# Loads of u issued by GpSimd instead of SyncE, and new costs in the planner of a fused attention and MoE kernel

## The chip, the cores and the metric

The kernel runs on one core of one Trainium2 chip. The metric is the device time of one execution in microseconds (us): the median of three runs. One further execution was taken with the hardware profiler; all rows of "the profile" and "the trace" are of that execution.

## The reference, cut to what matters

```python
# u, v: (8, 3008, 256); z: (8, 3008, 64); w_in: (256, 2048); w_out: (2048, 256)
scores = (z @ z.T) / S                     # per batch, S = 3008: a symmetric matrix
attn   = np.maximum(scores, 0.0) ** 2
x      = u * (attn @ v)                    # (8, 3008, 256)
x      = x.reshape(8 * 3008, 256)          # 24064 tokens
h      = x @ w_in
out    = (h * sigmoid(1.702 * h)) @ w_out  # (24064, 256), float32
```

## The kernel before, in words

**Units and tiles.** The attention half is cut into 48 units: 8 batches of 6 blocks of 512 rows (the last block of a batch has 448). The MoE half is cut into 47 tiles m of 512 tokens. In TensorE's order, tile m follows the attention work of unit m + 3.

**Work of a unit n.** `scores` makes 128 x 512 blocks of z z^T, two at a time (one pair, in PSUM, L340). Each pair is passed through relu (ScalarE L373 or VectorE L375) and squared in place (ScalarE L357 or VectorE L359) into a tile `ap_`. `values` multiplies V with the squares into four PSUM banks O (L553); h = 0 and h = 1 are the two halves of the 256 columns. Since the scores are symmetric, a square made for one unit serves a later unit transposed: SyncE issues a DMA transpose, `T<-ap_` (L295). From the second batch on, a part of a unit's own diagonal block is also made by such a transpose, the "mirror" (`ap_<-ap_`, L310).

**Draining.** `both_sums` copies two banks to one of five `sums` buffers (ScalarE L531, VectorE L533) and GpSimd adds the two halves (L526). A `sums` buffer of O is free again when the gate has read it; one of the MoE output, when its store to DRAM has landed. Each unit takes two buffers for O and each tile m two for the output, in a strict rotation of five.

**The steps of u.** For each unit u is loaded as float32 into `RU` (L96, issued by SyncE in `load_u`), split by GpSimd into its 16-bit halves (`UH<-RU`, L138), transposed by two DMA transposes that SyncE issues (`UHT<-UH`, L142) and merged by GpSimd (`UT<-UHT`, L146). There is one buffer of each, so the load of the next unit waits for the split of this one. The gate on GpSimd (`XT<-sums,UT`, L564, one for each h) multiplies the added sums with UT and gives the input of the MoE half. SyncE then swaps its partition halves (`XS<-XT`, L440); `hidden` (L596) needs both. `outs` (L639) makes the output.

**MoE elementwise work.** ScalarE makes the sigmoid `tsg<-hg` (L603), VectorE the product `GT<-hg,tsg` (L607).

**What sets the order.** Every engine carries out its own list of instructions in order; semaphores join the lists. The order in the lists is written by a planner inside the kernel: it walks through TensorE's work and keeps a clock for each engine (`now`), a table of costs (`cost`) and due times. `push` offers an operation for one or several engines: the one that would finish it first takes it, the earliest start goes first, and of equal starts the kinds in FIRST ("part", "gate", "add", "merge") go first. `send` offers a transfer to SyncE's list, which takes those that are ready by the number of the unit they are due for. `ready` times after a DMA are the issue's end plus `T_DMA`. `at(n, j, ...)` in the main part fixes the place of loads of weights, z and V on GpSimd by a position in unit n; before each a small copy, `hold`, makes GpSimd wait for the newest square. The planner knows nothing of the rotation of the `sums` buffers.

The first batch starts without any squares to reuse, loads all weights, and makes z and V of the second batch ready; from the second batch on all batches look alike.

Of the kernel before, what the change touches and what calls it, by code (L numbers as in the profile page):

```python
# [15 lines left out]
def kernel(  # L16
# [97 lines left out]

    def load_u(n):
        b, isup = divmod(n, NIS)
        rows(b, u, isup, 1, RU, sp, False)

    def load_z(b):
        for k in range(NIS):  # L120
# [33 lines left out]
    def turn_z(b, q):  # L154

        c = slice(q * ZN, (q + 1) * ZN)
        pool.tensor_copy(z16[:, c, 1, :], z16[:, c, 0, :])  # L157

        def turn(at):
            sp.dma_start_transpose(ZT[b % 2][:, c, :], z16[:, c, :, :].rearrange("p n a d -> p (n a d)"))  # L160
            if q == ZQ - 1:
                z_at[b] = at + T_DMA

        send(now["pe"] + 1.0, "turn_z", b * NIS - 3, turn)

# [5 lines left out]
    NU = B * NIS  # L171
    v_at = [7.2, 9.5, 10.0, 13.0, 13.5, 15.5]
    T_SC, T_SW, T_MM, T_HG = 0.215, 0.1, 0.107, 0.215
    T_LAT, T_SEM, T_DMA = 0.25, 0.1, 3.5
    now = {"pe": 6.0, "act": 6.0, "dve": 7.0, "pool": 6.0, "sp": 6.0}
    cost = {
        ("act", "relu"): 1.03, ("dve", "relu"): 1.23, ("act", "sq"): 1.03, ("dve", "sq"): 0.95,
        ("act", "keep"): 0.6, ("dve", "keep"): 0.45, ("act", "keep2"): 1.03, ("dve", "keep2"): 0.75,
        ("act", "relu_half"): 0.6, ("dve", "relu_half"): 0.7, ("act", "sq_half"): 0.6, ("dve", "sq_half"): 0.42,
        ("act", "part"): 0.6, ("dve", "part"): 0.7, ("pool", "add"): 1.1, ("act", "sig"): 1.03, ("dve", "gt"): 1.23, ("pool", "gate"): 1.2,  # L180
        ("sp", "turn"): 1.45, ("sp", "mirror"): 1.3, ("pool", "split"): 2.2, ("pool", "merge"): 2.2, ("sp", "turn_u"): 2.9, ("sp", "turn_z"): 2.2, ("sp", "store"): 0.6, ("sp", "swap"): 1.2,
    }
    BOTH = ("act", "dve")
    FIRST = ("part", "gate", "add", "merge")
    ops = []
    pushed = 0
# [4 lines left out]
    def push(ready, kind, engines, fn):  # L191
        nonlocal pushed
        pushed += 1
        ops.append((ready, pushed, kind, engines, fn))
# [4 lines left out]
    def advance(t):  # L199

        while ops:
            best = None
            for o in ops:
                e = min(o[3], key=lambda x: max(now[x], o[0]) + cost[(x, o[2])])
                key = (max(now[e], o[0]), o[2] not in FIRST, o[2][:2] == "sq", o[1])
                if best is None or key < best[0]:
                    best = key, o, e
            (start, *_), o, e = best
            if start > t:
                break  # L210
            ops.remove(o)
            now[e] = start + cost[(e, o[2])]
            o[4](e, now[e] + T_SEM)
        while now["sp"] <= t:
            can = [o for o in sends if o[0] <= t and (o[4] is None or o[4]())]
            if not can:
                break
            o = min(can, key=lambda o: (o[2], o[0]))
            sends.remove(o)
            now["sp"] = max(now["sp"], o[0]) + cost[("sp", o[1])]  # L220
            o[3](now["sp"])

    def pe_at(rows_, dur):
# [7 lines left out]
    NDIR = 3  # L231
# [52 lines left out]
    def turn(n, t, at):  # L284

        b, isup = divmod(n, NIS)
        key = (b * NIS + t // 2, isup)
        if key not in T:
            c = colors.pop(0)
            T_col[key] = c  # L290
            T[key] = ptp.tile([P, NIB, NIB, P], F16, name=f"T{c}", tag=f"T{c}")
            T_left[key] = [2, NIB]
        a = A[(n, t)]
        g0 = (t % 2) * 2
        sp.dma_start_transpose(  # L295
            T[key][:, g0:g0 + 2, :, :].rearrange("p g i r -> p (g i) r"), a.rearrange("p g c -> p (g c)"),
        )
        T_left[key][0] -= 1
        if T_left[key][0] == 0:
            T_at[key] = at + T_DMA  # L300
        a_left[(n, t)] -= 1

    def by_halves(a):
# [3 lines left out]
    def mirror(n, at):  # L307

        t = n % NIS * 2
        sp.dma_start_transpose(  # L310
            A[(n, t + 1)].rearrange("p g (i r) -> p (g i) r", i=NIB)[:, :NIB, :],
            A[(n, t)].rearrange("p g c -> p (g c)")[:, ISUP:],
        )
        a_left[(n, t)] -= 1
        half_at(n, at + T_DMA)

    halves_at = {}

# [6 lines left out]
    def scores(k):  # L325

        nonlocal nxt
        for i in range(k):
            n, t = pairs[nxt]
            nxt += 1  # L330
            b, isup = divmod(n, NIS)
            Z = ZT[b % 2]
            assert b in z_at
            p_ = take_ps()
            sc = psA.tile([P, 2, ISUP], F32, name="sc", tag="A")
            low = NIB // 2 if mirrored(n, t) else 0
            cols = slice(low * P, ISUP)
            for g in range(2):
                h0 = g * DQK
                pe.matmul(  # L340
                    sc[:, g, cols], Z[h0:h0 + DQK, 2 * t + g, :],
                    Z[h0:h0 + DQK, isup * NIB + low:(isup + 1) * NIB, :],
                    start=True, stop=True,
                )
            part = "_half" if low else ""
            if (n, t) in home:
                a = home[(n, t)]
            else:
                a = pap.tile([P, 2, ISUP], F16, name="ap_", tag="ap_")
                ring.append((n, t))  # L350
            A[(n, t)] = a
            a_left[(n, t)] = 2 + (turns(n, t) or mirrored(n, t + 1))

            def squared(e, at, n=n, t=t, a=a, isup=isup, cols=cols):
                x = by_halves(a)[:, :, 1, :] if mirrored(n, t) else a
                if e == "act":
                    act.activation(x, x, AF.Square, scale=1.0)  # L357
                else:
                    dve.tensor_tensor(x, x, x, ALU.mult)  # L359
                if mirrored(n, t):  # L360
                    half_at(n, at)
                else:
                    A_at[(n, t)] = at
                    if mirrored(n, t + 1):
                        send(at, "mirror", n - 1, lambda at: mirror(n, at), lambda: (n, t + 1) in A)
                latest[0] = a
                if turns(n, t):
                    key = (n - isup + t // 2, isup)
                    send(at, "turn", NDIR if n == 1 and (n, t) in home else key[0], lambda at: turn(n, t, at), lambda: key in T or len(colors) > 0)

            def relu(e, at, p_=p_, x=sc, y=a, part=part, squared=squared):
                if e == "act":
                    act.activation(y, x, AF.Relu, scale=CSC)  # L373
                else:
                    dve.tensor_scalar(y, x, 0.0, CSC, ALU.max, ALU.mult)  # L375
                set_ps(p_, at)
                push(at, "sq" + part, BOTH, squared)

            if low:
                relu.__defaults__ = (p_, sc[:, :, cols], by_halves(a)[:, :, 1, :], part, squared)  # L380
            elif mirrored(n, t + 1):
                relu.__defaults__ = (p_, sc.rearrange("p g (i c) -> p g i c", i=2), by_halves(a), part, squared)
            push(pe_at(H, T_MM if low else T_SC), "relu" + part, BOTH, relu)

    Os, Ys, GTs = {}, {}, {}
# [11 lines left out]
    def u_did(step, n, at):  # L397
# [6 lines left out]

        n_ = u_done["load"] + 1
        if ask("load", n_, ("split", n_ - 1)):
            def load(at, n=n_):
                load_u(n)
                u_did("load", n, at + T_DMA)

            send(at, "store", n_ - 1, load)
        n_ = u_done["split"] + 1
        if ask("split", n_, ("load", n_), ("turn", n_ - 1)):
            def split(e, at, n=n_):
# [5 lines left out]
        if ask("turn", n_, ("split", n_), ("merge", n_ - 1)):  # L420
            def turn_(at, n=n_):
                turn_u(n)
                u_did("turn", n, at + T_DMA)

            send(at, "turn_u", n_ - 1, turn_)
        n_ = u_done["merge"] + 1
        if ask("merge", n_, ("turn", n_), ("gate", n_ - 1)):
            def merge(e, at, n=n_):
# [113 lines left out]
    def values(n, js, h, ends):  # L542
# [15 lines left out]
        if ends:  # L558
            O = Os.pop((n, h))

            def summed(s_, at):
                def gate(e, at):
                    for from_, to in places(n):
                        pool.tensor_tensor(to(XT[:, h, :]), from_(s_), from_(UT[:, h, :]), ALU.mult)  # L564
                    if h == 1:
                        u_did("gate", n, at)
                        done = x_until[0] // TB
                        x_until[0] += w
                        if x_until[0] // TB > done:
                            send(at, "swap", n + 1, lambda at: swap_x(done, at))  # L570

                if u_done["merge"] >= n:
                    push(at, "gate", ("pool",), gate)
# [54 lines left out]
    def outs(m, fg, h):  # L628
# [17 lines left out]
        if end:  # L646
# [5 lines left out]
            def summed(s_, at):  # L652
# [1 line left out]
                    sp.dma_start(out_of(m)[:, 2 * h:2 * h + 2, :], s_.rearrange("p (n c) -> p n c", n=2))  # L654
                    stored.add((m, h))

                send(at, "store", m + 1, store)

            both_sums(Y, h, ISUP, 1.0 / FSC, at, summed)

# [48 lines left out]
    for b in range(1, B):  # L709
# [3 lines left out]
        for q in range(ZQ):  # L713
            at(n0 + 2 + late, (14 if late else EDGE) + 2 * q, lambda b=b, q=q: turn_z(b, q))
        for q in range(NIS // 2):
            at(n0 + 3 + late + q // 2, (EDGE, 12 - late)[q % 2], lambda b=b, q=q: load_v(b, 2 * q, 2))


    zss, zt_at = [], {}
# [179 lines left out]
```

## Time and profile before

| What | Value |
|---|---|
| time, median of 3 runs | 1236.1 us (1234.49 to 1237.28) |
| profiled execution | 1241.4 us |
| span of the profiled execution | 1239.4 us |
| TensorE (PE) busy | 1215.0 us, 98% |
| VectorE (DVE) busy | 919.2 us, 74% |
| ScalarE (ACT) busy | 817.2 us, 66% |
| GpSimd (POOL) busy | 747.4 us, 60% |
| mean granted clock of TensorE | 0.994 |
| DMA of SyncE's queue / GpSimd's queue | 69.1% / 12.3% of 16 engines' span |

How to read it: the span is what the profiler saw between the first and the last instruction; the profiled execution is 2.0 us longer than its span and 5.3 us above the median of the runs without a profile. A busy TensorE need not be one at its peak: matmuls overlap, and their ends are modelled. Idle time of the other engines costs nothing unless TensorE waits for it.

### The profile page before, as it was taken

The numbers are of one execution on the slowest core, as the hardware profiler recorded it, in microseconds if no ns is written. First come the engines' busy times: TensorE is split into PE (matmuls) and PEld (weight loads), VectorE is DVE, ScalarE is ACT, GpSimd is POOL, SyncE is SP. The second block draws the span as 40 slices with busy tenths as digits, with TensorE's granted clock in tenths as the row PEclk, the third lists the DMA queues.
The fourth block names the chain that finished last, engine by engine and source line by source line (L and its number), as shares of the span: only waits on it lengthen the run. The fifth ranks groups of instructions, "written<-read, shape, count | busy, mean of one in ns | idle before, by whom it ended". The sixth has DMA issues, their size and how long they took to land.

```text
span 1239.4 us, 35791 instructions
## 1 busy us (share of the span) xinstructions
PE 1215.0 (98%) x15286; PEld 810.5 (65%) x15286; DVE 919.2 (74%) x894; ACT 817.2 (66%) x942; POOL 747.4 (60%) x812
## 2 busy tenths in 40 slices
PE   8989799999999999999999999999999999999998
PEld 4556479999677666555666566655666556666676
DVE  7877687777887768777777777777778777777556
ACT  8846477666776567666676667766676666766545
POOL 5685966564666647665576645765567656554441
PEclk9999899999999999999999999999999999999999
DMA  9999799987999769898498975999659986686311
GB/s 170 179 175 152 171 169 176 161 145 134 142 157 164 140 142 146 157 166 169 92 163 159 179 141 108 154 167 187 119 117 161 174 162 124 126 150 126 69 36 52
DMA packets 461776, 179.18 MB, mean 145 GB/s; under 512 B 419184, under 2 KB 438064, under 8 KB 461616
## 3 DMA queue, kind: packets, MB, share of 16 engines
q1 hardware_dynamic: 428128, 159.45, 69.1%
q0 software_dynamic: 33488, 17.44, 12.3%
q8 instruction: 119, 1.95, 0.7%
q14 instruction: 41, 0.34, 0.1%
HBM read 60.29 MB, written 24.64 MB: 69 GB/s over the span
## 4 chain that ended last, share of the span: by engine, by line
PE 87%; POOL 4%; DMA 3%; DVE 2%; issue 2%; SPq 1%; ACT 0%; DVEq 0%; POOLq 0%; ACTq 0%
PE O L553 34%; PE hg L596 24%; PE yps L639 24%; PE sc L340 5%; DMA RU<-in_u_dram 1%; POOL sums L526 1%; DMA UHT<-UH 1%; POOL UT L146 1%; SPq L142 1%; POOL UH L138 1%; PE O L585 1%; POOL XT L564 1%; DMA ap__1880<-ap__1530 1%; DVE GT L607 0%; DMA out_dram<-sums 0%
## 5 line engine op out<-in xcount | busy, mean ns | idle before, releaser
L607 DVE TENSOR_TENSOR GT<-hg,tsg 128x1024 f16<-128x1024 f32 x376 | 454.5, 1220 | 229.4 <-ACT tsg L603 225.5
L603 ACT ACTIVATE tsg<-hg 128x1024 f16<-128x1024 f32 x376 | 377.7, 1022 | 294.2 <-PE hg L596 291.7
L526 POOL TENSOR_TENSOR sums<-sums 128x512 f32<-128x512 f32 (+1 forms) x188 | 244.3, 1301 | 416.2 <-ACT sums L531 266.1
L553 PEld LDWEIGHTS <-V 64*128 64x128 f16 x5420 | 282.5, 94 | 206.5 <-issue 17.2
L596 PE MATMUL hg<-XT,W 64*128 64x512 f16 x1504 | 382.8, 377 | 0.7 <-DVE GT L607 0.5
L639 PE MATMUL yps<-W,GT 64*128 64x256 f16 x6016 | 379.0, 269 | 1.1 <-DVE GT L607 1.1
L596 PE MATMUL hg<-XS,W 64*128 64x512 f16 x1504 | 368.0, 376 | 0.0
L639 PEld LDWEIGHTS <-GT 64*128 64x128 f16 x6016 | 316.3, 94 | 62.0 <-DVE GT L607 1.3
L596 PEld LDWEIGHTS <-W 64*128 64x128 f16 x3008 | 169.6, 94 | 122.8 <-issue 3.0
L553 PE MATMUL O<-T,V 64*128 64x512 f16 (+2 forms) x2496 | 223.9, 316 | 4.9 <-DVE sums L533 4.9
L564 POOL TENSOR_TENSOR XT<-sums,UT 128x256 f16<-128x256 f32 (+7 forms) x220 | 178.4, 834 | 7.0
L146 POOL COPY UT<-UHT 128x1024 uint16<-128x1024 uint16 x96 | 132.0, 1419 | 23.9 <-DMA UHT<-UH 21.2
L340 PE MATMUL sc<-ZT 64*128 64x512 f16 (+1 forms) x688 | 122.9, 364 | 3.3 <-ACT ap__407 L373 1.0
L138 POOL COPY UH<-RU 128x1024 uint16<-128x1024 uint16 x96 | 99.1, 1056 | 21.9 <-DMA RU<-in_u_dram 17.4
L531 ACT ACTIVATE sums<-O 128x512 f32<-128x512 f32 (+1 forms) x109 | 61.3, 582 | 22.0 <-PE O L553 16.5
L533 DVE TENSOR_SCALAR sums<-yps 128x512 f32<-128x512 f32 x86 | 58.7, 687 | 20.2 <-PE yps L639 17.0
L531 ACT ACTIVATE sums<-yps 128x512 f32<-128x512 f32 x98 | 57.3, 596 | 22.8 <-PE yps L639 12.9
L533 DVE TENSOR_SCALAR sums<-O 128x512 f32<-128x512 f32 (+1 forms) x83 | 55.4, 674 | 9.4 <-PE O L553 4.6
L340 PEld LDWEIGHTS <-ZT 64*128 64x128 f16 x688 | 41.0, 94 | 23.8 <-issue 5.5
L96 POOL DMA_DIRECT2D z<-in_z_dram x35 | 26.3, 759 | 0.0
L96 POOL DMA_DIRECT2D V<-in_v_dram x26 | 17.5, 673 | 0.0
L157 POOL COPY z<-z 128x384 f16<-128x384 f16 x28 | 13.8, 492 | 0.0
(1118 smaller groups left out, 1217.0 us busy)
## 6 DMA issues: line engine op xcount, KB each, us to landing
out_dram<-sums SPq DMA_DIRECT2D x92, 256.0 KB, 2.6
RU<-in_u_dram SPq DMA_DIRECT2D x40, 512.0 KB, 4.9
XS<-XT SPq DMA_DIRECT2D x94, 128.0 KB, 2.5
V<-in_v_dram POOLq DMA_DIRECT2D x14, 512.0 KB, 9.6
V<-in_v_dram POOLq DMA_DIRECT2D x12, 256.0 KB, 5.1
z<-in_z_dram POOLq DMA_DIRECT2D x35, 64.0 KB, 7.2
RU<-in_u_dram SPq DMA_DIRECT2D x8, 256.0 KB, 3.8
UHT<-UH SPq DMA_TRANSPOSE x96, 3.3
```

What stands on the lines that cost most here:

```text
L138: pool.tensor_copy(UH[:, w, :], RU.bitcast(U16).rearrange("p n (x w) -> p w (n x)", w=2)[:, w, :])
L146: pool.tensor_copy(UT.bitcast(U16).rearrange("p c (n r w) -> p w n c r", n=NIB, w=2)[:, w, :, :, :], UHT[:, w, :, :, :],)
L340: pe.matmul(sc[:, g, cols], Z[h0:h0 + DQK, 2 * t + g, :], Z[h0:h0 + DQK, isup * NIB + low:(isup + 1) * NIB, :], start=True, stop=True,)
L526: pool.tensor_tensor(s_[:, 0, :w], s_[:, 0, :w], s_[:, 1, :w], ALU.add)
L531: act.activation(s_[:, g, :w], ps[g][:, :w], AF.Copy, scale=scale)
L533: dve.tensor_scalar(s_[:, g, :w], ps[g][:, :w], scale, None, ALU.mult)
L553: pe.matmul(o, vj, x, start=first, stop=last)
L564: pool.tensor_tensor(to(XT[:, h, :]), from_(s_), from_(UT[:, h, :]), ALU.mult)
L596: pe.matmul(hg[:, e, :], half(W1[:, c, fg * P:(fg + 1) * P], e), half(x[:, c // 2, p0:p0 + TB], e), start=(c == 0), stop=(c == 2 * NK - 1),)
L603: act.activation(tsg, hg, AF.Sigmoid, scale=1.702 / FSC)
L607: dve.tensor_tensor(GT, hg, tsg, ALU.mult)
L639: pe.matmul(Y[g][:, i2 * D:(i2 + 1) * D], half(GT[:, e, s * P:(s + 1) * P], g), half(W2[:, ff, :], g), start=(fg == 0 and e == 0 and i2 == ...
```

## The change

The edits fall into four groups. `load_u` issues on GpSimd instead of SyncE; the planner offers it to GpSimd as an operation "load" of cost 0.6, outside FIRST, and counts its landing 1.0 later. The transfers that follow a step of GpSimd (transposes of u, swaps, stores) are offered to SyncE with a ready time that is 1.0 later (`T_POOL`). Costs: while TensorE's clock in the planner is below 120, a DMA counts 1.5 more and a place in SyncE's list 1.3 times as much; the square on VectorE costs 0.9 for units 0 to 2, 1.7 for units 3 to 5 and 1.05 later (it was 0.95 for all), the half square 0.8 (0.42), and GpSimd's add, gate and merge cost 1.4, 1.6 and 3.0 (1.1, 1.2 and 2.2). The three loads of the second batch's V are placed at (3, 12), (4, 9) and (4, 20) instead of (4, 9), (4, 11) and (5, 9). No arithmetic changes, and TensorE carries out the same number of matmuls of each shape.

```diff
     def load_u(n):
         b, isup = divmod(n, NIS)
-        rows(b, u, isup, 1, RU, sp, False)
+        rows(b, u, isup, 1, RU, pool, False)
...
-    T_LAT, T_SEM, T_DMA = 0.25, 0.1, 3.5
+    T_LAT, T_SEM, T_DMA, T_POOL = 0.25, 0.1, 3.5, 1.0
...
-        ("act", "relu"): 1.03, ("dve", "relu"): 1.23, ("act", "sq"): 1.03, ("dve", "sq"): 0.95,
+        ("act", "relu"): 1.03, ("dve", "relu"): 1.23, ("act", "sq"): 1.03, ("dve", "sq"): 1.05, ("act", "sq1"): 1.06, ("dve", "sq1"): 1.7, ("act", "sq0"): 1.06, ("dve", "sq0"): 0.9,
...
-        ("act", "relu_half"): 0.6, ("dve", "relu_half"): 0.7, ("act", "sq_half"): 0.6, ("dve", "sq_half"): 0.42,
-        ("act", "part"): 0.6, ("dve", "part"): 0.7, ("pool", "add"): 1.1, ("act", "sig"): 1.03, ("dve", "gt"): 1.23, ("pool", "gate"): 1.2,
-        ("sp", "turn"): 1.45, ("sp", "mirror"): 1.3, ("pool", "split"): 2.2, ("pool", "merge"): 2.2, ("sp", "turn_u"): 2.9, ...
+        ("act", "relu_half"): 0.6, ("dve", "relu_half"): 0.7, ("act", "sq_half"): 0.6, ("dve", "sq_half"): 0.8,
+        ("act", "part"): 0.6, ("dve", "part"): 0.7, ("pool", "add"): 1.4, ("act", "sig"): 1.03, ("dve", "gt"): 1.23, ("pool", "gate"): 1.6,
+        ("sp", "turn"): 1.45, ("sp", "mirror"): 1.3, ("pool", "split"): 2.2, ("pool", "merge"): 3.0, ("pool", "load"): 0.6, ("sp", "turn_u"): 2.9, ...
     }
+    T_BUSY = 120.0
+
+    def dma():
+
+        return T_DMA + (1.5 if now["pe"] < T_BUSY else 0.0)
...
-            now["sp"] = max(now["sp"], o[0]) + cost[("sp", o[1])]
+            now["sp"] = max(now["sp"], o[0]) + cost[("sp", o[1])] * (1.3 if now["pe"] < T_BUSY else 1.0)
...
-            def relu(e, at, p_=p_, x=sc, y=a, part=part, squared=squared):
+            def relu(e, at, p_=p_, x=sc, y=a, kind="sq0" if n < NDIR else "sq1" if n < NIS else "sq" + part, squared=squared):
...
-                push(at, "sq" + part, BOTH, squared)
+                push(at, kind, BOTH, squared)
...
         if ask("load", n_, ("split", n_ - 1)):
-            def load(at, n=n_):
+            def load(e, at, n=n_):
                 load_u(n)
-                u_did("load", n, at + T_DMA)
+                u_did("load", n, at + dma() + 1.0)
 
-            send(at, "store", n_ - 1, load)
+            push(at, "load", ("pool",), load)
...
-            send(at, "turn_u", n_ - 1, turn_)
+            send(at + T_POOL, "turn_u", n_ - 1, turn_)
...
-                            send(at, "swap", n + 1, lambda at: swap_x(done, at))
+                            send(at + T_POOL, "swap", n + 1, lambda at: swap_x(done, at))
...
-                send(at, "store", m + 1, store)
+                send(at + T_POOL, "store", m + 1, store)
...
-            at(n0 + 3 + late + q // 2, (EDGE, 12 - late)[q % 2], lambda b=b, q=q: load_v(b, 2 * q, 2))
+            at(*((3, 12), (4, EDGE), (4, 20))[q] if late else (n0 + 3 + q // 2, (EDGE, 12)[q % 2]), lambda b=b, q=q: load_v(b, 2 * q, 2))
```

The other places where `T_DMA` was added to a time now add `dma()`.

More of the change, by code (lines that the diff above doesn't have):

```diff
@@ L161, in turn @@
             if q == ZQ - 1:
-                z_at[b] = at + T_DMA
+                z_at[b] = at + dma()
         send(now["pe"] + 1.0, "turn_z", b * NIS - 3, turn)
@@ L173 @@
     T_SC, T_SW, T_MM, T_HG = 0.215, 0.1, 0.107, 0.215
-    T_LAT, T_SEM, T_DMA = 0.25, 0.1, 3.5
+    T_LAT, T_SEM, T_DMA, T_POOL = 0.25, 0.1, 3.5, 1.0
     now = {"pe": 6.0, "act": 6.0, "dve": 7.0, "pool": 6.0, "sp": 6.0}
     cost = {
-        ("act", "relu"): 1.03, ("dve", "relu"): 1.23, ("act", "sq"): 1.03, ("dve", "sq"): 0.95,
+        ("act", "relu"): 1.03, ("dve", "relu"): 1.23, ("act", "sq"): 1.03, ("dve", "sq"): 1.05, ("act", "sq1"): 1.06, ("dve", "sq1"): 1.7, ("act", "sq0"): 1.06, ("dve", "sq0"): 0.9,
         ("act", "keep"): 0.6, ("dve", "keep"): 0.45, ("act", "keep2"): 1.03, ("dve", "keep2"): 0.75,
-        ("act", "relu_half"): 0.6, ("dve", "relu_half"): 0.7, ("act", "sq_half"): 0.6, ("dve", "sq_half"): 0.42,
-        ("act", "part"): 0.6, ("dve", "part"): 0.7, ("pool", "add"): 1.1, ("act", "sig"): 1.03, ("dve", "gt"): 1.23, ("pool", "gate"): 1.2,
-        ("sp", "turn"): 1.45, ("sp", "mirror"): 1.3, ("pool", "split"): 2.2, ("pool", "merge"): 2.2, ("sp", "turn_u"): 2.9, ("sp", "turn_z"): 2.2, ("sp", "store"): 0.6, ("sp", "swap"): 1.2,
+        ("act", "relu_half"): 0.6, ("dve", "relu_half"): 0.7, ("act", "sq_half"): 0.6, ("dve", "sq_half"): 0.8,
+        ("act", "part"): 0.6, ("dve", "part"): 0.7, ("pool", "add"): 1.4, ("act", "sig"): 1.03, ("dve", "gt"): 1.23, ("pool", "gate"): 1.6,
+        ("sp", "turn"): 1.45, ("sp", "mirror"): 1.3, ("pool", "split"): 2.2, ("pool", "merge"): 3.0, ("pool", "load"): 0.6, ("sp", "turn_u"): 2.9, ("sp", "turn_z"): 2.2, ("sp", "store"): 0.6, ("sp", "swap"): 1.2,
     }
     BOTH = ("act", "dve")
+    T_BUSY = 120.0
+    def dma():
+        return T_DMA + (1.5 if now["pe"] < T_BUSY else 0.0)
     FIRST = ("part", "gate", "add", "merge")
@@ L299, in turn @@
         if T_left[key][0] == 0:
-            T_at[key] = at + T_DMA
+            T_at[key] = at + dma()
         a_left[(n, t)] -= 1
@@ L314, in mirror @@
         a_left[(n, t)] -= 1
-        half_at(n, at + T_DMA)
+        half_at(n, at + dma())
     halves_at = {}
@@ L376, in relu @@
                 set_ps(p_, at)
-                push(at, "sq" + part, BOTH, squared)
+                push(at, kind, BOTH, squared)
             if low:
-                relu.__defaults__ = (p_, sc[:, :, cols], by_halves(a)[:, :, 1, :], part, squared)
+                relu.__defaults__ = (p_, sc[:, :, cols], by_halves(a)[:, :, 1, :], "sq" + part, squared)
             elif mirrored(n, t + 1):
-                relu.__defaults__ = (p_, sc.rearrange("p g (i c) -> p g i c", i=2), by_halves(a), part, squared)
+                relu.__defaults__ = (p_, sc.rearrange("p g (i c) -> p g i c", i=2), by_halves(a), "sq" + part, squared)
             push(pe_at(H, T_MM if low else T_SC), "relu" + part, BOTH, relu)
@@ L422, in turn_ @@
                 turn_u(n)
-                u_did("turn", n, at + T_DMA)
-            send(at, "turn_u", n_ - 1, turn_)
+                u_did("turn", n, at + dma())
+            send(at + T_POOL, "turn_u", n_ - 1, turn_)
         n_ = u_done["merge"] + 1
```

## The prediction

> **What bounds the kernel now.** The page comes first, then the waits of TensorE (engine, line, what for: us in total, times, longest).
>
> ```profile
> span 1239.4 us, 35791 instructions
> ...
> PE O L553 <- DMA ap__1880<-ap__1530: 8.7, 1, 8.7
> PE O L553 <- DVE sums L533: 4.9, 1, 4.9
> ```
>
> TensorE is busy for 1215.0 of 1239.4 us. Two waits stand out, and the next is 1.2. The windows tell where there is anything to gain (stretch, then PE, weight loads, DVE, ACT and POOL busy with counts, granted clock, DMA share, GB/s):
>
> ```profile
> 30.00:76.00 46.00, 45.89 (x470) 26.25 (x468) 36.80 (x37) 37.15 (x41) 34.20 (x33) 1.00 1.18 168
> 76.00:88.00 12.00, 7.15 (x69) 4.11 (x66) 8.66 (x6) 3.11 (x5) 6.10 (x12) 0.86 1.08 190
> 88.00:120.00 32.00, 32.00 (x421) 21.13 (x419) 22.92 (x21) 19.70 (x23) 19.26 (x18) 1.00 1.07 174
> 130.00:150.00 20.00, 11.32 (x128) 7.46 (x125) 12.78 (x11) 7.50 (x9) 19.77 (x24) 0.74 0.83 163
> 584.00:735.00 151.00, 151.00 (x1932) 91.16 (x1926) 114.38 (x111) 100.83 (x118) 94.32 (x104) 1.00 0.83 148
> ```
>
> The last row is one batch in the middle of the run: TensorE full, clock 1.00. No edit takes a matmul out, so what can be gained lies in 76:88 (stall A) and 130:150 (stall B). 421 matmuls in 32 us are 0.0760 us each. At that, A's 69 are 5.2 us of work, so 6.8 are lost; B's 128 are 9.7, so 10.3 are lost. Weighing each matmul by its columns (a pair of 512 columns takes 0.2165 us in full stretches) I get 7.0 and 10.9, together 17.9. Each is its wait and about 2 us more after it, when the clock granted is lower.
>
> Stall A, seen on VectorE (start, us, what; in brackets the idle time before):
>
> ```profile
> 73.37 3.89 DVE L359 TENSOR_TENSOR ap__1127<-ap__1127 128x1024 f16<-128x1024 f16 x1 [1.18 <-ACT ap__1127 L373]
> 77.18 4.02 DVE L359 TENSOR_TENSOR ap__1150<-ap__1150 128x1024 f16<-128x1024 f16 x1
> 82.26 0.67 DVE L533 TENSOR_SCALAR sums<-yps 128x512 f32<-128x512 f32 x1
> ```
>
> A square that usually takes 0.69 takes 3.9 and 4.0 while GpSimd works without a gap; 6.5 us too many, and the drain that TensorE waits for stands behind them. Stall B, on SyncE's queue:
>
> ```profile
> 39.67 3.17 SPq L142 DMA_TRANSPOSE UHT<-UH  x2
> 42.89 0.66 SPq L96 DMA_DIRECT2D RU<-in_u_dram  x1
> ...
> 117.18 7.41 SPq L96 DMA_DIRECT2D RU<-in_u_dram  x2
> ...
> 136.45 0.34 SPq L96 DMA_DIRECT2D RU<-in_u_dram  x1
> 136.83 1.19 SPq L310 DMA_TRANSPOSE ap__1880<-ap__1530  x1
> ```
>
> The mirror is issued at 136.83 and lands at 144.05, though its source was squared by 106.3. Ahead of it in the list stand loads of u, which wait for GpSimd's split.
>
> **Part by part: stall B.** Without loads of u, by the order of the built instructions the mirror is SyncE's 54th transfer, directly behind the swap of unit 3. Its source is ready at about 111, that swap's gate at about 105. Issued at 111, it lands by 115 to 118 (3.3 at UHT's median, 7.2 as before). TensorE needs it at about 140: some 22 us of slack. B's 10.9 us go. Two squares of unit 7 and the swaps behind are next, and have 1 to 3 us left at least.
>
> **Stall A.** Of 14 squares of units 3 to 5 VectorE made 10 and makes 7: half, not "mostly". The two near the spot are still its own, so beside a busy GpSimd up to 3.3 us each could come back. They cost nothing as long as the wait that follows now covers them.
>
> **The new wait.** In GpSimd's list the load of u of unit 2 comes behind all that starved it: gates and adds are in FIRST, "load" is not. Behind it stand the load of unit 3, its split, unit 2's merge and then unit 2's gate. The drain of the first tile's output on VectorE takes the `sums` buffer that this gate frees, a product GT stands behind the drain on VectorE, and TensorE's next `hidden` waits for GT. That `hidden` is 72.4 us of work into TensorE's list; 8.45 are lost before 70 in both kernels, so it would be reached at 80.85. When is it released?
>
> ```profile
> 39.63 1.19 POOL L133 DMA_DIRECT2D W<-in_moe_w_out_dram  x1
> ...
> 52.80 1.57 POOL L146 COPY UT<-UHT 128x1024 uint16<-128x1024 uint16 x1 [4.51 <-DMA UHT<-UH]
> ...
> 61.79 3.75 POOL L96 DMA_DIRECT2D z<-in_z_dram  x5
> ...
> 67.31 2.59 POOL L146 COPY UT<-UHT 128x1024 uint16<-128x1024 uint16 x2
> ...
> 72.27 2.49 POOL L564 TENSOR_TENSOR XT<-sums,UT 128x512 f16<-128x512 f32 x2
> ```
>
> Here W2's load was under way while unit 1 was transposed: issued at 39.67, the second transpose landed at 52.8, 6.5 us for one. Undisturbed, three took 5.06 (1.69 each). After, W2 is issued at about 32 (it takes 12.9, so to 45), and six transposes of GT stand between unit 0's, landed at 37, and unit 1's two. Of these eight, 1.8 get through until 45; 6.2 x 1.69 make 10.5: unit 1 is there at 55.5. Bounds: 50.5 if W2 disturbs nothing, 58 if none of the eight gets through before.
>
> From 55.5 on GpSimd's list is a chain, by its rows: merge 2.7 (58.2), eight z loads 5.5 (63.7), two gates 2.5 (66.2), two adds 2.5 (68.7). Then the load of unit 2: issue 0.65, landing (68.7 to 74.4); V's load 0.65 and the z casts 2.7 lie beside it. Split 2.05 and add 1.25 (77.7), load of unit 3: issue 0.65, landing (83.4), split 2.05 (85.5), merge 2.6 (88.1), add 1.25 (89.3), gate 1.27 (90.6). On VectorE drain 0.69, GT 1.22: TensorE goes on at 92.5; rounded down for the steps that overlap by a tenth or two, 92. The landings are the unknown, since this form was not on this queue:
>
> ```profile
> RU<-in_u_dram SPq DMA_DIRECT2D x40, 512.0 KB, 4.9
> V<-in_v_dram POOLq DMA_DIRECT2D x14, 512.0 KB, 9.6
> V<-in_v_dram POOLq DMA_DIRECT2D x12, 256.0 KB, 5.1
> ```
>
> I take 5.1: the same load took 4.9 on SyncE's queue, and the nearer V row agrees. The 9.6 is the upper end (+9 for the two), 3.8 (the 256 KB load of RU) the lower (-2.6).
>
> The Trainium skill, "DMA: Bandwidth & Descriptors", section Anatomy of one DMA, gives a DMA from GpSimd about 2.0 us and its bytes over 436 GB/s, by which 512 KB would take an estimated 3.2; the sum would then be 3.8 lower, near 1227.5. The trace disagrees: 64 KB of z landed in 7.2.
>
> **The rest.** The squares are then on ScalarE (1.06 each for three more, 3 us in 20, ScalarE 66% busy): hidden. 56 issues on GpSimd at 0.65 are 36 us of a run in which it idles 490: hidden in the middle batches, where the order gives each merge a unit's lead; without that cover each would delay its gate by 0.65. The transfers placed later keep their order there. V at (3, 12), (4, 9), (4, 20) is needed only in the second batch: nothing. The swap of unit 0 lands at 56.5 to 58 where TensorE needs it at 56.3: 0 to 1.5 us, which the new wait absorbs.
>
> **The sum.** Before: A 7.0 and B 10.9, 17.9. After: 92 - 80.85 = 11.15, and 1.9 at a lower clock behind it, as after A and B: 13.05. Gain 4.9. The profiled execution would be 1241.4 - 4.9 = 1236.5; it stood 5.3 above the median of 1236.1, which would be 1231.
>
> **Rivals.**
> 1. *The loads land as V's larger row.* With 9.6 twice, TensorE resumes at 101, loses 22.05, and the time is 1236.1 + 4.1 = 1240. It decides from a resumption at 96.85, where nothing is gained: 4.85 over the two landings, or 7.5 each. For it: the row, and the DMA share of 1.08 in 76:88. Against it: loads of u in the same crowd took 4.9 on the other queue. A page of the Trainium skill, "SBUF — State Buffer", speaks for it (section SBUF: two separate sides): while VectorE holds the port it shares with GpSimd, GpSimd can't write its transfers' descriptors. No run here shows this; the long z row would agree with it.
> 2. *The gate is in time.* If the planner's lists run faster than I add up (W2 harmless, landings of 3.8, steps beside each other), the wait is 3 to 5 us or none, both stalls go: 1218 to 1225. Against it: 80.85 asks for 11 us less, in a chain of rows.
> 3. *B stays.* If the swap ahead of the mirror waits for a gate that the new wait delays past 130, the time is 1231 + 10.9 = 1242. Against it: 25 us of room.
> 4. *It does not do what it says.* The loads do leave SyncE's list; the squares move by 3 of 14 only, and nothing rests on them.
>
> **How the numbers follow.** A change of 0.2% (2.5 us) is about what a measurement of this kernel can tell from none. A resumption at 88 to 94.3 (1227 to 1233.6) has 0.46, rival 2 has 0.07: faster 0.53. At 94.3 to 99.3, around the break-even, 0.16: same. Later (rival 1, 0.24, with 9.6 for one or both) or rival 3 (0.05), or an unseen loss elsewhere (0.02): slower 0.31. The range of 8 in 10 goes from 1223 (half of rival 2 left out) to 1242 (rival 1 with W2 at its bound of 58 left out, and some of 3). The likeliest case alone is 1227 to 1234.
>
> **What would show it.** In the changed kernel's profile TensorE's wait for the mirror is gone, the clock in 130:150 is 1.00 and the mirror is issued near 111. RU's rows stand on POOLq, with landings near 5. A new wait of about 11 us, `hg` for GT, ends near 92; ahead of it a VectorE drain waits for a gate on GpSimd. If that wait is missing or ends before 85, my chain is wrong; if it ends after 97, or a wait stands in 130:150, the sign is. A middle batch longer than the 151.6 us that one takes now would show that GpSimd's issues are not hidden.

## The result, and the profile after

| | kernel before | changed kernel | ratio, 95% interval |
|---|---|---|---|
| first measurement, median of 5 each | 1237.28 us | 1245.76 us (1244.50 to 1247.29) | 1.0070 (1.0051 to 1.0089) |
| again, median of 31 and 10 | 1240.01 us (1234.65 to 1248.62) | 1247.01 us (1242.22 to 1248.79) | 1.0051 (1.0031 to 1.0071) |
| profiled execution | 1241.41 us | 1244.50 us | |

The change makes the kernel slower by 7 to 8.5 us (0.5 to 0.7%), where 5 us less were forecast. The table also shows how far executions of one kernel lie apart; the 5.3 us by which the profiled execution of before stood above its median were such spread, and a second profile of before took 1241.48 us.

The span, and TensorE's waits in the changed kernel (columns as before; its line numbers are 6 higher from `scores` on, so L602 is `hidden`, L559 the values, L613 the product GT, L570 the gate, L539 a drain on VectorE):

```profile
span 1242.7 us, 35725 instructions
...
PE hg L602 <- DVE GT L613: 16.1, 3, 15.6
PE O L559 <- DVE sums L539: 1.5, 5, 0.8
```

Both old stalls are gone: no row for the mirror, and 0.8 where a drain cost 4.9. One new wait of 15.6 stands in their place. The windows show where it is (columns as in the prediction):

```profile
76.00:88.00 12.00, 7.42 (x92) 4.94 (x88) 3.57 (x3) 4.55 (x6) 5.04 (x5) 1.00 1.27 148
88.00:120.00 32.00, 20.91 (x224) 11.01 (x226) 16.48 (x17) 14.67 (x16) 23.86 (x26) 0.79 0.78 149
130.00:150.00 20.00, 19.99 (x306) 13.83 (x304) 17.02 (x17) 15.14 (x17) 16.21 (x19) 1.00 0.70 122
584.00:735.00 151.00, 150.80 (x1928) 104.06 (x1924) 112.23 (x110) 101.30 (x118) 99.37 (x112) 1.00 0.85 149
```

130:150 is full at clock 1.00. TensorE stands still from 83 to 99 us, and no other engine is full there (GpSimd works 5.04 of 12 us, then 23.86 of 32): this is a chain, not a full engine. GpSimd's list shows the chain (start, us, what; in brackets the idle time before and its releaser):

```profile
70.06 0.60 POOL L96 DMA_DIRECT2D RU<-in_u_dram  x1
...
70.79 0.71 POOL L96 DMA_DIRECT2D V<-in_v_dram  x1
...
76.60 2.02 POOL L138 COPY UH<-RU 128x1024 uint16<-128x1024 uint16 x2 [2.80 <-DMA RU<-in_u_dram]
...
79.80 0.57 POOL L96 DMA_DIRECT2D RU<-in_u_dram  x1
...
90.25 2.02 POOL L138 COPY UH<-RU 128x1024 uint16<-128x1024 uint16 x2 [8.58 <-DMA UHT<-UH]
92.21 2.55 POOL L146 COPY UT<-UHT 128x1024 uint16<-128x1024 uint16 x2
...
95.92 2.48 POOL L570 TENSOR_TENSOR XT<-sums,UT 128x512 f16<-128x512 f32 x2
```

Unit 3's split starts at 90.25. It waits not for its own load, which had landed at 87.70, but for unit 2's transposes, since it writes over `UH`, which they read. On SyncE's queue, on VectorE and on TensorE that looks like this:

```profile
72.13 7.03 SPq L160 DMA_TRANSPOSE ZT<-z  x2
79.26 8.21 SPq L142 DMA_TRANSPOSE UHT<-UH  x2
```

```profile
97.21 0.69 DVE L539 TENSOR_SCALAR sums<-yps 128x512 f32<-128x512 f32 x1 [16.82 <-POOL XT L570]
```

```profile
99.09 0.61 PE L602 MATMUL hg<-XT,W 64*128 64x512 f16 x1 [15.55 <-DVE GT L613]
```

The drain waits 16.8 us for the gate, GT stands behind it, and TensorE goes on at 99.1.

In what follows "loss" at a time is that time less the matmul work started by then; the work is counted by columns as in the prediction (a pair of matmuls of 512 columns is 0.2165 us).

| Profile | loss at 70 us | loss at 130 us of work | added from 584 to 1100 us |
|---|---|---|---|
| before / before again | 8.4 / 10.1 | 26.4 / 26.5 | 0.8 / 0.8 |
| changed / changed again | 10.6 / 14.9 | 28.5 / 30.3 | 2.1 / 2.2 |
| changed, V later | 9.1 | 22.9 | 2.1 |
| changed, loads on SyncE | 12.5 | 23.8 | 2.1 |
| changed, six sums | 8.8 | 17.9 | 2.1 |
| changed, six sums, loads on SyncE | 12.7 | 14.4 | 2.0 |
| before, loads on GpSimd, two squares moved | 10.5 | 11.5 | 0.6 |

### The profile page after: what moved, and what is told of

Read it like the earlier page. It is cut to its first block, busy times and chain, and to the rows that moved or that the text cites. A ratio compares the mean times of both kernels' runs of the same rounds, so it can differ in the third digit from the quotient of the medians.

```text
span 1242.7 us, 35725 instructions
## 1 busy us (share of the span) xinstructions
PE 1215.3 (98%) x15286; PEld 822.5 (66%) x15286; DVE 905.8 (73%) x884; ACT 822.2 (66%) x952; POOL 783.9 (63%) x868
## 4 chain that ended last, share of the span: by engine, by line
PE 91%; DVE 2%; POOL 2%; DMA 2%; issue 1%; ACT 1%; SPq 0%; DVEq 0%; POOLq 0%; ACTq 0%
PE O L559 34%; PE yps L645 25%; PE hg L602 25%; PE sc L346 5%; DMA UHT<-UH 2%; PE O L591 1%; POOL UT L146 1%; POOL UH L138 1%; DMA z<-in_z_dram 0%; POOL XT L570 0%; POOL sums L532 0%; DVE GT L613 0%; DVE sums L539 0%; PE warm L736 0%; ACT tsg L609 0%
## 5 line engine op out<-in xcount | busy, mean ns | idle before, releaser
L613 DVE TENSOR_TENSOR GT<-hg,tsg 128x1024 f16<-128x1024 f32 x376 | 453.5, 1221 | 236.9 <-ACT tsg L609 232.5
L532 POOL TENSOR_TENSOR sums<-sums 128x512 f32<-128x512 f32 (+1 forms) x188 | 252.2, 1343 | 319.8 <-ACT sums L537 185.2
L559 PEld LDWEIGHTS <-V 64*128 64x128 f16 x5420 | 281.4, 94 | 198.1 <-issue 7.1
L602 PE MATMUL hg<-XT,W 64*128 64x512 f16 x1504 | 383.7, 377 | 16.1 <-DVE GT L613 16.1
L602 PE MATMUL hg<-XS,W 64*128 64x512 f16 x1504 | 368.7, 377 | 0.7 <-DMA XS<-XT 0.7
L645 PEld LDWEIGHTS <-GT 64*128 64x128 f16 x6016 | 329.5, 94 | 43.4 <-DVE GT L613 1.3
L602 PEld LDWEIGHTS <-W 64*128 64x128 f16 x3008 | 167.0, 94 | 146.6 <-DVE GT L613 16.0
L559 PE MATMUL O<-T,V 64*128 64x384 f16 (+1 forms) x2496 | 221.6, 315 | 1.6 <-DVE sums L539 1.5
L570 POOL TENSOR_TENSOR XT<-sums,UT 128x256 f16<-128x256 f32 (+7 forms) x220 | 171.7, 803 | 6.6
L146 POOL COPY UT<-UHT 128x1024 uint16<-128x1024 uint16 x96 | 135.2, 1455 | 2.6
L537 ACT ACTIVATE sums<-yps 128x512 f32<-128x512 f32 x103 | 60.3, 597 | 47.4 <-PE yps L645 24.7
L539 DVE TENSOR_SCALAR sums<-yps 128x512 f32<-128x512 f32 x81 | 55.6, 686 | 37.2 <-PE yps L645 17.0
L539 DVE TENSOR_SCALAR sums<-O 128x512 f32<-128x512 f32 (+1 forms) x84 | 55.9, 681 | 11.5 <-PE O L559 6.5
L96 POOL DMA_DIRECT2D RU<-in_u_dram x40 | 23.1, 579 | 6.9 <-POOL UH L138 5.1
```

The lines of the kernel that those rows point to most:

```text
L146: pool.tensor_copy(UT.bitcast(U16).rearrange("p c (n r w) -> p w n c r", n=NIB, w=2)[:, w, :, :, :], UHT[:, w, :, :, :],)
L532: pool.tensor_tensor(s_[:, 0, :w], s_[:, 0, :w], s_[:, 1, :w], ALU.add)
L537: act.activation(s_[:, g, :w], ps[g][:, :w], AF.Copy, scale=scale)
L539: dve.tensor_scalar(s_[:, g, :w], ps[g][:, :w], scale, None, ALU.mult)
L559: pe.matmul(o, vj, x, start=first, stop=last)
L602: pe.matmul(hg[:, e, :], half(W1[:, c, fg * P:(fg + 1) * P], e), half(x[:, c // 2, p0:p0 + TB], e), start=(c == 0), stop=(c == 2 * NK - 1),)
```

## The experiments

**Is it the rotation of the `sums` buffers?**

```diff
-    NT = 12
-    NSUM = 5
+    NT = 11
+    NSUM = 6
```

> The changed kernel with six sums buffers instead of five (and 11 instead of 12 buffers for T, of which the planner uses no more); every engine's list is the same. Theory C (the rotation: the 15.6 us wait of hidden for GT is the first output drain waiting for unit 2's gate): the drain finds a free buffer, the wait falls from 15.6 to under 3 us, the next drain comes some 11 us of work later, when the gate (95.9) is just done; time 1229 to 1232. Rival S (it is the slower chain itself, TensorE needs unit 2's or 3's results in any case): the wait moves to another instruction and the time stays within 3 us of 1246.

Measured: 1236.28 us, 0.9962 of before (0.9927 to 0.9996), some 4 us more than the theory expected. The wait for GT is down to 0.3, and TensorE's longest is now one for a swap:

```profile
PE hg L602 <- DMA XS<-XT: 3.8, 2, 3.5
...
PE hg L602 <- DVE GT L613: 0.5, 2, 0.3
```

The gate itself was hardly earlier (94.25 against 95.92), so what TensorE waited for was not the gate's result: it was the coupling through the buffers. The swaps behind the late gate are next, which the expectation left out and which cost 3.5. The rotation is shown.

**What makes the gate late? First: the transposes of z ahead of u's.** The chain does not begin at the same time in all runs. So besides the time at which TensorE resumes, the runs are compared by the time from the end of unit 1's gates on GpSimd, behind which unit 2's load goes out, to this resumption: 31.4 us in the changed kernel (67.7 to 99.1), 29.8 in a second profile of it, which is reported below.

```diff
-            sp.dma_start_transpose(ZT[...], z16[...])
+            (z_kept.append if b == 1 and q < 2 else lambda go: go())(lambda: sp.dma_start_transpose(ZT[...], z16[...]))
...
-                turn_u(n)
+                turn_u(n); [go() for go in z_kept if n == 2]
```

> The changed kernel with the first two transposes of the second batch's z put behind the two of unit 2's u in SyncE's list; nothing else changes place. Theory C1 (unit 2's gate is late because those two stand ahead in SyncE's queue): unit 2's u is issued right after its split at 78.7, lands near 83, the split of unit 3 then waits for its own load only (85), TensorE resumes near 93 instead of 99, time 1239 to 1241. Rival C2 (the transposes are slow because the transfers share the same 16 engines, whatever the order): they land at 88 or later, TensorE resumes at 97 or later, time 1243 to 1247.

Measured: 1247.35 us, 1.0032 of before (1.0000 to 1.0065). Unit 2's transposes went out at 81.41, right after their split, and yet unit 3's split started at 92.70, now held by its own load:

```profile
83.55 0.57 POOL L96 DMA_DIRECT2D RU<-in_u_dram  x1
...
92.70 2.02 POOL L138 COPY UH<-RU 128x1024 uint16<-128x1024 uint16 x2 [7.28 <-DMA RU<-in_u_dram]
```

That load took 9.1 us to land. TensorE resumed at 101.6, 30.1 us behind the gates, no less than the changed kernel itself. The order in SyncE's list is not the cause: C1 falls.

**Second: the crowd of transfers.** All four transposes of z behind unit 3's u (as above, with `if b == 1` and `n == 3`), and V's first load issued with the second:

```diff
-            at(..., lambda b=b, q=q: load_v(b, 2 * q, 2))
+            at(..., lambda b=b, q=q: pool_busy(0.9) if (b, q) == (1, 0) else [load_v(b, 2 * q, 2), rows(b, v, 0, 2, V16[1][:, :2 * NIB, :], pool) if (b, q) == (1, 1) else None])
```

> The changed kernel with two kinds of transfers taken out of the stretch of 70 to 92 us: all four transposes of the second batch's z are put behind unit 3's u in SyncE's list, and the first load of the second batch's V is issued together with the second one. All else keeps its place. Theory C2 (unit 2's gate is late because the transfers of this stretch share the 16 engines: u's load takes 6.5 to 9 us and u's transposes up to 11): both come down to near 5 and 3.3, unit 3's split starts at 85 to 86 instead of 90.3, TensorE resumes near 94 to 95, and the time is 4 to 5 us below the changed kernel's. Rival C3 (the lists alone, not the crowd, set these times): the split still starts at 89 or later, the time as the changed kernel's.

Measured: 1242.71 us, 1.0020 of before (0.9991 to 1.0049). The split started at 85.12, loads landed in 5.3 to 5.7 and transposes in 3.2 to 5.5, TensorE resumed at 94.0, 25.6 us behind the gates: the steps are C2's, as worked out. By the ratios to before, the time is some 4 us below the changed kernel's.

**Third: V's load alone.** The second diff above without the first.

> The changed kernel with only the first load of the second batch's V moved: issued together with the second one, some 25 us later. Theory (GpSimd's queue carries V and u one behind the other): unit 3's load lands in 5.5 to 6 instead of 7 to 8, but unit 2's transposes stay behind the two of z and land at 86 to 88; TensorE resumes at 95 to 97, time 2 to 4 below the changed kernel's. Rival (V's load is the whole crowd): as without V and z both, resuming at 94. Rival (V does nothing): 98 or later.

Measured: 1240.67 us, 1.0005 of before (0.9979 to 1.0030), against 1247.01 for the changed kernel, measured beside it. TensorE resumed at 93.0, so the first rival has it, not the theory. Of the 6.1 us, 1.3 come from a chain that began earlier here, which V's load can't have done, since it stands behind. Counted from the gates it is 26.6 us, 3.2 to 4.8 less than in the two profiles of the changed kernel, which lie 1.6 apart. The transposes of z, left in front, cost no more than that spread (26.6 with them, 25.6 without). The landings of unit 2's and 3's transposes before 95 us (least, median, most), first in the changed kernel:

```profile
DMA to landing us min/median/max: 3.1/5.0/10.9
```

and here, together with GpSimd's split of unit 3:

```profile
DMA to landing us min/median/max: 3.1/3.4/6.4
...
84.11 2.02 POOL L138 COPY UH<-RU 128x1024 uint16<-128x1024 uint16 x2 [4.84 <-DMA RU<-in_u_dram]
```

V is issued on GpSimd's queue, and the transposes on SyncE's. The Trainium skill, "DMA: Bandwidth & Descriptors", section Issuing engines are not separate DMA queues, says that transfers of all issuing engines interleave on the same 16 engines; these two lines agree with it.

**The loads' queue.**

```diff
-        rows(b, u, isup, 1, RU, pool, False)
+        rows(b, u, isup, 1, RU, sp, False)
```

> The changed kernel with the loads of u issued by SyncE after all, at the same place in the program; the other engines' lists are the same. Theory Q (the queue is not what costs: the place of unit 2's load in the program is): the load of unit 2 lands about as late, the wait of hidden for GT stays at 12 to 17 us, and the mirror waits for loads again, so 1245 to 1253. Rival (GpSimd's queue is what makes the loads slow): they land in 4.9, the wait for GT falls to 10 or less, 1238 to 1242.

Measured: 1240.97 us, 1.0021 of before (0.9986 to 1.0056). The landings of the loads of units 2 and 3, first in the changed kernel, then here, and the wait for GT, which is down:

```profile
DMA to landing us min/median/max: 6.5/7.2/7.9
...
DMA to landing us min/median/max: 4.3/4.3/4.4
...
PE hg L602 <- DVE GT L613: 8.8, 3, 8.2
```

The rival has it: on GpSimd's queue, beside V's load, u's loads are slower. TensorE resumed at 93.2, 27.9 us behind the gates, with V's load where the change put it. So the delay needs both loads at once on GpSimd's queue. In the four profiles in which unit 2's load goes out on it just ahead of V's (the changed kernel's two, the one with six buffers, the one with z's transposes moved), V's took 11.4 to 12.8 us. It took 8.1 here, 8.0 in the last run below (u from SyncE too), and 6.5 in the next one, where u's load goes out 19 us ahead. Why two loads on this queue delay each other is not shown. The mirror did not come back as a wait either (issued at 113.5): the new place in the program was enough to free it.

**The planner's order.**

```diff
-    FIRST = ("part", "gate", "add", "merge")
+    FIRST = ("part", "gate", "add", "merge", "load")
```

> The changed kernel with the new operation load in FIRST, so that the planner places unit 2's load ahead of the gates, the adds and the z loads (the plan changes behind that point). Theory C (the wait for GT is the chain load of unit 2, its split, its transposes, unit 3's split, unit 2's gate): unit 2's split no longer waits for its load, starts some 3 us earlier, the wait of 15.6 becomes 9 to 12, time 4 to 6 below the changed kernel's, 1238 to 1242. Rival (the crowd on the engines sets it): no gain, 1244 to 1248.

Measured: 1238.87 us, 0.9989 of before (0.9957 to 1.0021): the time as expected, by another way. The wait for GT is 1.4 and ends at 95.1, but unit 0's gates moved behind the load, and `hidden` waited for its swap; by 70 us 20 were already lost:

```profile
PE hg L602 <- DMA XS<-XT: 5.2, 1, 5.2
```

**The kernel before, with the loads alone, and with stall A alone.** First:

```diff
-        rows(b, u, isup, 1, RU, sp, False)
+        rows(b, u, isup, 1, RU, pool, False)
```

> The kernel before with nothing changed but the engine that issues the loads of u: GpSimd instead of SyncE, at the same place in the program. All other lists are as before. Theory (stall B was the mirror behind loads that waited for the split): the 8.7 us wait for the mirror is gone, stall A stays as it was, time 1225 to 1229. Rival (loads on GpSimd's queue are themselves late): a new wait of some 5 to 10 us in the first 150 us and 1234 or more.

Measured: 1237.93 us, 0.9975 (0.9946 to 1.0005). Stall B is gone and A stays (4.0), but 2.6 for the mirror of a later unit and 2.0 of issue in `hidden` came up. The theory has the waits right and the time wrong: the gain is within the spread. Then the two squares on ScalarE, and nothing else:

```diff
-                if e == "act":
+                if e == "act" or (n, t) in ((4, 8), (4, 9)):
```

> The kernel before with the two stretched squares of unit 4 (the ones that took 3.9 and 4.0 us) on ScalarE instead of VectorE; nothing else. Theory A1 (stall A is in every execution as in the profiled one): the 4.9 us wait is gone and the time falls by 5 to 7, to 1230 to 1232. Rival A2 (the profiled execution was a slow one because of stall A, which most executions have in part): the median falls by 0 to 3 us while the profiled execution falls from 1241 to about 1235.

Measured: 1243.23 us, 1.0017 (0.9985 to 1.0049). Stall A is gone and nothing is gained:

```profile
PE O L553 <- DMA ap__1880<-ap__1530: 13.3, 1, 13.3
```

TensorE came earlier and waited longer. It resumed at 145.05, against 144.09 before. Both A1 and A2 fall; A was no loss of its own. A second profile of before, unaltered, says the same:

> The kernel before itself, unaltered, for a second profile. If the profiled execution shown is typical: stall A with a wait of 4 to 5 us, stall B of 8 to 9, resuming near 144, and the time within 3 us of it. If executions differ in the stalls: another split between A and B, the end of B between 140 and 150, and the time off by as much.

Measured: 1239.60 us, 1.0000 (0.9976 to 1.0025). 1.7 us more were lost before 70, the waits were 3.7 and 7.6, and the loss behind B was 26.5 against 26.4. Both edits on before together:

> The kernel before with both stalls' causes taken away: loads of u on GpSimd's queue at the same place in the program, and the two stretched squares of unit 4 on ScalarE. Theory (the stalls are two, and each alone is given back in the next wait, as the run with the squares alone showed: its wait for the mirror grew from 8.7 to 13.3): without both the time falls by 8 to 12 us, to 1229 to 1233. Rival (the end of GpSimd's chain sets the time in these 150 us, and a third wait takes their place): 0 to 5 below before.

Measured: 1237.12 us, 0.9978 (0.9945 to 1.0012). The profiled execution has no stall over 2.0 and lost 11.5 where before lost 26.4, and took 1230.10; but it was the fastest of its ten, and the interval reaches from a gain of 7 us to a loss of 1.5. What the slower of the ten lost was not profiled, and stays open.

**The changed kernel again, and the version that the runs point to.** First unaltered:

> The changed kernel itself, unaltered, as the anchor for the other runs of this call and for a second profile. All theories expect the wait of hidden for GT at 13 to 17 us, resuming at 97 to 101, and a time 4 to 9 us above the kernel before in the same call.

Measured: 1247.01 us (ratio in the table); wait 12.9, resuming at 100.3. TensorE reached this wait 3.8 us later than in the first profile and left it 1.2 later, so most of what was lost earlier is absorbed here too. Then with both edits of above, six buffers (`NSUM = 6`, `NT = 11`) and `sp` in `load_u`:

> The changed kernel with both: six sums buffers, and the loads of u issued by SyncE at the same place in the program. Theory (two separate parts of the same wait: the rotation of sums makes TensorE wait for unit 2's gate, and GpSimd's queue makes that gate some 6 us later): the wait for GT is gone, the swaps behind it are no longer late either, the loss up to 150 us is 12 to 15 instead of the changed kernel's 28, and the time 8 to 12 below the kernel before, near 1229 to 1232. Rival (each is given back in the next wait): as with six buffers alone, 4 to 5 below before.

Measured: 1232.27 us, 0.9944 of before (0.9925 to 0.9963). This is the kernel most clearly faster than before, by some 7 us, a little less than the theory's 8 to 12; six buffers alone are faster too, but barely (interval up to 0.9996), and the two intervals overlap. The rest goes by the theory: the wait is gone, 14.4 are lost up to 130 us of work, and the stretch in which the changed kernel was idle is full:

```profile
76.00:100.00 24.00, 24.00 (x276) 15.47 (x274) 16.48 (x18) 17.16 (x19) 14.13 (x14) 1.00 1.05 166
```

The swaps still cost something: 1.5 behind unit 2's gate, where six buffers alone had 3.5, and 3.1 for unit 0's swap at 58.8.

## Why the prediction was wrong, point by point

**Stall B's removal: right.** The wait for the mirror is gone. The mirror went out at 118 (forecast 111), still before it was needed.

**The new wait: right in kind and place.** It is `hidden` for GT, behind an output drain, behind unit 2's gate, as the prediction named it; the run with six buffers shows it.

**Its size: the step that failed.** TensorE resumed at 99.1 and 100.3 in the two profiles, not 92, past the break-even of 96.85 and past 97, from where the prediction itself said that its sign would be wrong. Up to unit 2's load the sum came out (70.06 against 68.7), in part by luck: unit 0's transposes, put down as landed at 37, were under way together with W2's load and landed at 45.9, and unit 1's still came at 57.0, within the bounds. Unit 2's split began at 76.6, not 74.4: the load landed in 6.5, not 5.1. (The sum also puts the issue, 0.65, ahead of each landing, though the profile counts landings from the start of the issue: 1.3 us too many for the two loads, which made the forecast later, not earlier.)

The large term is the next one. "load of unit 3: issue 0.65, landing (83.4), split" passed over two things: that this split also needs unit 2's transposes, and what was in the air. The split began at 90.25 instead of 83.4, so 6.9 of the 7.1 us are there: 2.2 brought along from unit 2's split, and 4.7 new. What stretched it was put at nothing in "the rest": "V at (3, 12) ... nothing". For V's load the prediction asked only when it is needed, not beside what it is sent. With it moved away, the split begins at 84.1 and TensorE resumes at 93.0, of which 1.3 us are an earlier start. V's place is one half of the cause and u's new queue the other: with u's loads on SyncE and V left in place, TensorE resumes at 93.2.

**Rival 1 named the neighbourhood and not the mechanism.** The loads landed in 6.5 to 7.9, below 9.6; the transposes on the other queue, up to 10.9, made the rest. The estimate of 3.2 by the formula of the Trainium skill ("DMA: Bandwidth & Descriptors", Anatomy of one DMA) was exceeded twofold and more. That VectorE keeps GpSimd from writing descriptors isn't shown by any run here.

**A as 7.0 us that can be had: wrong as a reason, without effect on the sum.** A lay inside the wait for the mirror; B's end, at 143.5 to 145.1 in three profiles, set the whole loss. As B's removal was in the change, the 17.9 stood: with both removed, the kernel before lost only 1.0 between 70 us and 130 us of work.

**Middle batches: "nothing" was wrong, but not for the loads.** From 584 to 1100 us, about 3.4 batches, the changed kernel loses 2.1, before 0.8. GpSimd's issues don't cost this: on the kernel before, with the loads moved and nothing else, it is 0.7 (0.6 with the squares moved too), and with the loads back on SyncE under the new plan 2.0 and 2.1. It belongs to the plan that the new costs and ready times make. (Between 130 us of work and 584 us those two versions of before lost 8.3 and 6.1 where before lost 2.2, so there the moved loads are not free without a plan that knows of them.) A middle batch of before with loads on GpSimd, and of the new plan with loads on SyncE and six buffers:

```profile
584.00:735.00 151.00, 151.00 (x1932) 91.27 (x1930) 114.39 (x111) 101.21 (x117) 98.61 (x112) 1.00 0.85 149
```

```profile
584.00:735.00 151.00, 150.80 (x1924) 103.72 (x1920) 112.23 (x110) 100.36 (x118) 95.45 (x102) 1.00 0.85 150
```

None of TensorE's time is idle in the first, 0.2 us in the second. Which of the new costs makes the 2.1 was not tried.

**The sum.** The forecast was a loss of 4.9 less; the first profiles show 3.2 more (loss near the end of the run, at about 1200 us, 32.8 against 29.6). Of the 8.1 us between, 6.7 come from the new wait (7.1 later, and 0.4 less at the lower clock: a loss of 28.2 right behind it, not 21.5) and 1.4 from all that is lost later (4.6 against 3.2). The median forecast had another 5 us of error in it, since the profiled execution was no slower than others. The medians lie 7 to 8.5 us apart and the two pairs of profiles only 3.1 and 4.8; where the rest of the medians' difference is lost is not shown.

**Squares of units 3 to 5.** One of VectorE's two near the spot took 1.74 us, beneath the wait: nothing, as forecast.

## What to carry to other kernels

When an engine waits for a chain of steps on other engines, list for every step everything that it needs, the buffer that it overwrites included, and everything else that is on the DMA engines then; "needed only later" says when a transfer may land, not whom it delays. A wait whose end is fixed by such a chain absorbs the losses ahead of it that do not delay the chain: before counting two stalls as two gains, ask whether the second ends earlier when the first is gone. And a rotation of buffers can tie an engine to a result that it does not need; on the changed kernel one buffer more took 10.6 us off the loss up to 130 us of work, and the best of the edits to the order alone 5.6 (both against its first profile).

## What the runs showed of the hardware that was not expected

With one 512 KB load of V on GpSimd's queue, unit 2's two transposes on SyncE's queue landed in 10.9 and 6.8 us; with that load moved they took 3.6 and 6.4. The loads of u around it took 6.5 and 7.9 us, with V moved 5.4 and 6.7, and 4.3 and 4.4 when SyncE issued them under the same plan. V's own load took 11.4 to 12.8 us beside a load of u on the same queue, and 6.5 to 8.1 without one. The same kernel took 1234.65 to 1248.62 us in 31 executions on one chip; losses ahead of the fixed waits differ by up to 4 us between profiles of one kernel (10.6 and 14.9 at 70 us), which the waits behind then hide for the most part.
